# A transformer block on one Trainium2 core: the list schedule behind the attention starts 2.1 slots later, and its rule and table of numbers change

## The chip, the cores and the metric

The kernel runs on one core of a Trainium2 chip. The core has five engines with instruction queues of their own: TensorE (PE) for matmuls, VectorE (DVE), ScalarE (ACT), GpSimd (POOL) and SyncE (SP), which here does nothing but issue transfers (DMA). Each engine works through its queue in the order in which the program was written down, and waits at an instruction until what it needs is there. So the order of instructions on each engine is fixed before the kernel runs, and the order is what this change alters.

The metric is the device time of one execution in microseconds (us); lower is better. Three executions of the kernel before took 988.43, 991.43 and 991.93 us, median 991.43.

## The reference

The input x has 2048 rows of 512 numbers. What is computed, with 32 heads of 16 and a window of 256:

```python
mod = (_silu(c) @ w_mod).reshape(c.shape[0], 6, 1, -1)
sa, ca, ga, sb, cb, gb = (mod[:, 0], ..., mod[:, 5])
h = _layernorm(x) * (1 + ca) + sa
q, k, v = ...  # h @ wqkv, split into 32 heads of 16
scores = jnp.einsum("bhqd,bhkd->bhqk", q, k) * (Dh ** -0.5)
mask = (idx[:, None] - idx[None, :] >= 0) & (idx[:, None] - idx[None, :] < W)
p = _softmax(jnp.where(mask, scores, -1e9))
x = x + ga * (einsum("bhqk,bhkd->bhqd", p, v) @ wo)
h = _layernorm(x) * (1 + cb) + sb
x = x + gb * ((_silu(h @ w1) * (h @ w3)) @ w2)      # w1, w3: 512 x 1792, w2: 1792 x 512
```

All of it is float32. The kernel splits an operand into a high and a low part, and a product of two such operands is three matmuls.

## The kernel before, in words

**Attention.** 32 units of work, four heads and one block of 512 query rows each. Unit u is spread over stages: `unit_a` multiplies the normalised rows by the weights of queries and keys (L433), mixes high and low parts on GpSimd (L451) and writes the result through SyncE into a ring of rows laid out for the scores (`ring<-qk`, L456, six transfers of 128 KB). `unit_b` makes a first set of scores (`mx<-ring`, L486), finds each row's maximum on VectorE (L493 to L502), turns it (L508) and puts it into the ring (`ring<-mT`, L517). `unit_c` makes the scores again with the maximum subtracted (L736, L739), applies exponential and mask (L744 to L785), multiplies by the values (L712) and stores the output (`o_dr<-os`, L804). The stages of neighbouring units overlap; a unit takes eight slots of the plan, and a hand-written table gives each step's place in slots. The last unit is number 31; its six row transfers stand at slots 231.45 to 231.79.

**Behind the attention**, for four blocks of 512 rows: `o_sums` loads softmax sums (L1051), takes reciprocals (L1055) and writes them (L1056). `o_part` loads an output tile (L1075) and the spread reciprocals (L1070), multiplies (L1087) and splits into high and low (L1079, L1082). `o_proj` multiplies by the output weights (L1099) and `add_stats` adds x and gathers statistics (L968 to L976). `load_x1` fetches x (L1036), `load_wo` the output weights (L1030). Then the second layer norm (`ln_rstd` L987 to L993, `ln2` L1219 with turns on TensorE L1233).

**Feed-forward.** Two halves of the rows, seven steps each. A step has 14 up products (`ffn`, L1361, six matmuls each; fourteen since the 2 x 2 x 2 block products are done by seven), elementwise work on ACT, VectorE and GpSimd (L1384 to L1413), and 8 down products (L1454). The step's weights are loaded by `load_w` (L1157) and `load_w2` (L1200) and split (ACT L952, GpSimd L953). Each down step overwrites the one down-weight buffer, so the next load of it starts after the last down product of the step before. `half_rows` (L1294, L1302) and `late_job` (L862, L1173, L1187) prepare work for later steps on the side.

**What sets the order.** All steps of the attention with a place below `TS`, in slots, are issued in the order of the places. The others, `fixed`, enter the list scheduler `Sched` at a time `us(t)`; the work behind the attention enters it as operations with an engine, a cost, dependencies and a priority (`key`) that comes from the table `K`. `Sched.deal` takes, at each step, for the engine that is free first, the ready operation of the lowest key. Of `fixed` the row transfers are `urgent`: a transfer `o` that would run when an urgent one is due is put off. `CAPS` limits how many result banks turns (`tp`), up (`up`) and down products (`dn`) may hold at a time. Three things in `K` choose the engine of an instruction (`be`, `by`) and a count per block (`n`); all else are keys and shifts of keys in us, such as `fl`, the distance between steps of the feed-forward, and `w0`, the key of the first weights' load.

```python
    last = [o for o in ops if o[0] >= TS]
    fixed = [(us(t), fn, *KINDS[kind]) for t, _, fn, kind in last]
    urgent = [us(t) for t, _, _, kind in last if kind in ("rows", "qk_rows")]
```

Of the kernel before, what the change touches and what calls it, by code (L numbers as in the profile page):

```python
# [36 lines left out]
         o=(9.93, 10.63), job=(-0.855, 2.493, 10.058))  # L37
# [26 lines left out]
HOP = {"PE": 0.42, "ACT": 0.2, "DVE": 0.15, "POOL": 0.1, "SP": 0.0, "NIL": 0.0}  # L64
SWITCH = 0.2
STRETCH = 3.413
CAPS = dict(tp=1, up=5, dn=5)


def act(n):  # L70
# [39 lines left out]
class Sched:  # L110
# [36 lines left out]
    def deal(self):  # L147
# [4 lines left out]
        mode, wire, lanes, clock = 0, 0.0, [0.0] * 8, Clock()  # L152
        banks, fixed = list(self.banks), list(self.fixed)
        held = dict.fromkeys(CAPS, 0)
        given = dict.fromkeys(CAPS, 0)
        order, self.dealt = [], []
# [8 lines left out]
        while left:  # L165
            best = None
            for e, lst in ready.items():
                t, pick = free[e], None
                for key, seq, o in lst:
                    s = o.est  # L170
                    new = [b for b in o.bank if b.i is None]
                    if new:
                        use = new[0].use
                        if held[use] >= CAPS[use] or (use in INORDER and new[0].n != given[use]):
                            continue
                        at = min(banks)
                        if at == INF:
                            continue
                        s = max(s, at)
                    if o.kb:  # L180

                        b = max(s, t)
                        end = max(wire, b + 1.5) + o.kb / RATE + o.more - QUIET
                        s = max([s] + [u + 0.01 for u in self.urgent if b <= u < end])
                    if s <= t:
                        pick = (t, o)
                        break
                    if pick is None or s < pick[0]:
                        pick = (s, o)
                if pick and (best is None or pick[0] < best[0]):  # L190
                    best = pick
            if fixed and (best is None or fixed[0][0] <= best[0]):

                t, e = max(free[fixed[0][2]], fixed[0][0]), fixed[0][2]
# [7 lines left out]
            elif fixed and (best is None or fixed[0][0] <= best[0]):  # L202
                t, fn, e, occ = fixed.pop(0)
# [5 lines left out]
            s, o = best  # L209
# [11 lines left out]
            if o.kb:  # L221
                s = max(s, lanes.pop(0))
                wire = max(wire, s + 1.5) + o.kb / RATE + o.more
# [29 lines left out]
INF = float("inf")  # L253
RATE = 320.0

QUIET = 1.5
KEY = 1.715
TS = 229.9


def us(t):

    return KEY * (min(t, TW[0]) - TS + TW[2] * max(0.0, min(t, TW[1]) - TW[0]) + TW[3] * max(0.0, t - TW[1]))


TW = (231.0, 241.0, 0.8, 0.65)

KINDS = dict(product=("PE", 0.235), mix=("POOL", 1.25), qk_rows=("SP", 1.2), out=("ACT", 0.5), job=("POOL", 2.0),
             job_dma=("SP", 0.5), scores=("PE", 0.2), top=("DVE", 0.5), parts=("DVE", 0.4), turn=("PE", 0.11), cut=("ACT", 0.16),
# [6 lines left out]

BY = ((("POOL", "POOL"),) * 3 + (("DVE", "DVE"),), (("POOL", "POOL"),) * 3 + (("DVE", "DVE"),),
      (("POOL", "DVE"),) * 3 + (("DVE", "DVE"),), (("POOL", "POOL"),) * 4)
K = dict(be=(('DVE', 'DVE'), ('DVE', 'POOL'), ('DVE', 'POOL'), ('POOL', 'POOL'), ('POOL', 'DVE'),
         ('POOL', 'DVE'), ('DVE', 'DVE')), hr=0.109, de=7.098, wo=-0.159, x1=5.764, xb=-29.382,  # L280
         xl=0.241, os=-0.129, ol=(-15.316, -4.484, -6.572, 4.956), pl=(3.999, 1.87, -4.828,
         102.62), pe=(0.982, -5.962, 56.258, 232.622), o=(1.381, 8.497, 20.124, -0.531), n=(1, 1,
         2, 1), w0=62.113, l2=0.424, f=1.543, fl=40.897, by=((('POOL', 'POOL'), ('DVE', 'DVE'),
         ('DVE', 'POOL'), ('DVE', 'DVE')), (('DVE', 'DVE'), ('DVE', 'POOL'), ('DVE', 'DVE'),
         ('DVE', 'POOL')), (('POOL', 'POOL'), ('POOL', 'DVE'), ('DVE', 'POOL'), ('POOL', 'DVE')),
         (('POOL', 'DVE'), ('DVE', 'POOL'), ('DVE', 'POOL'), ('DVE', 'POOL'))), w=0.559, dn=1.412,
         ds=0.003, l3=-0.027)
@with_exitstack
def block_kernel(ctx: ExitStack, tc: tile.TileContext, x, wqk, wv, wo, w13, w2, c, wmod, out):
    nc = tc.nc  # L290
# [1299 lines left out]
```

## Time and profile before

| | |
|---|---|
| executions | 988.43, 991.43, 991.93 us; median 991.43 |
| profiled execution | 987.77 us, its span 986.0 us |
| TensorE busy | 944.6 us (96%) |
| VectorE, ScalarE, GpSimd busy | 717.9, 554.2, 609.8 us |
| transferred | 141.64 MB, 144 GB/s on the mean |
| granted TensorE clock | 0.990 on the mean |

In rows of the profile, the first number is the start in us from the span's start, the second the busy time of the row, then engine, line, operation, and `out<-in` by the program's names; xN says that N instructions are joined. What stands in square brackets is idle time of the engine just before, and what ended it. SPq is SyncE's queue issuing a transfer; its time is that of issuing, not of the transfer. PEld is the loading of weights into TensorE. The rows of stretches give for each engine the busy time in the stretch, then the granted clock, the share of the DMA engines that was busy, and GB/s. Rows of waits give the total, the count and the longest, in us.

### The profile page before, as it was taken

The numbers are of one execution on the slowest core, as the hardware profiler recorded it, in microseconds if no ns is written. First come the engines' busy times: TensorE is split into PE (matmuls) and PEld (weight loads), VectorE is DVE, ScalarE is ACT, GpSimd is POOL, SyncE is SP. The second block draws the span as 40 slices with busy tenths as digits, with TensorE's granted clock in tenths as the row PEclk, the third lists the DMA queues.
The fourth block names the chain that finished last, engine by engine and source line by source line (L and its number), as shares of the span: only waits on it lengthen the run. The fifth ranks groups of instructions, "written<-read, shape, count | busy, mean of one in ns | idle before, by whom it ended". The sixth has DMA issues, their size and how long they took to land.

```text
span 986.0 us, 17173 instructions
## 1 busy us (share of the span) xinstructions
PE 944.6 (96%) x5316; PEld 717.4 (73%) x5316; DVE 717.9 (73%) x1999; ACT 554.2 (56%) x1252; POOL 609.8 (62%) x775
## 2 busy tenths in 40 slices
PE   5999999999999999997888999999999999999998
PEld 2578777777777776764566778878888888888886
DVE  7775889899989999996467676755568655555455
ACT  3433887787878787874577864333445344433330
POOL 7441787787868686864476588897737555443420
PEclk9999999999999999997999999999999999999999
DMA  8621354444544444435891558765336423312102
GB/s 280 189 87 34 125 187 142 142 141 142 177 150 148 145 150 143 142 131 152 218 268 68 175 169 285 235 206 192 121 96 208 147 73 96 96 59 81 38 22 85
DMA packets 80671, 141.64 MB, mean 144 GB/s; under 512 B 9538, under 2 KB 22338, under 8 KB 80580
## 3 DMA queue, kind: packets, MB, share of 16 engines
q1 hardware_dynamic: 79860, 139.50, 43.8%
q10 hardware_dynamic: 720, 1.05, 0.3%
q8 instruction: 42, 0.69, 0.3%
q14 instruction: 49, 0.40, 0.1%
HBM read 85.72 MB, written 34.61 MB: 122 GB/s over the span
## 4 chain that ended last, share of the span: by engine, by line
PE 74%; POOL 8%; DVE 7%; DMA 6%; issue 2%; ACT 2%; SPq 1%; POOLq 0%; DVEq 0%; ACTq 0%
PE mx L1361 11%; PE st L1361 11%; PE mx L486 8%; PE pj L433 7%; PE st L736 7%; PE st L1454 6%; PE po L712 6%; PE mx L1454 6%; PE pj L1361 4%; PE st L650 3%; PE pj L1454 2%; POOL w L953 2%; POOL pt L764 2%; POOL qk L451 1%; DMA ring<-qk 1%
## 5 line engine op out<-in xcount | busy, mean ns | idle before, releaser
L493 DVE CUSTOM_DVE_ANT_0 junk<-mx,mskq 128x384 bf16<-128x384 f32 (+2 forms) x512 | 256.5, 527 | 35.4 <-PE mx L486 34.1
L953 POOL TENSOR_TENSOR w<-w,w 128x512 fp32r<-128x512 f32 (+2 forms) x56 | 107.7, 1936 | 124.4 <-ACT w L952 93.4
L486 PE MATMUL mx<-ring 96*128 96x384 f32 (+2 forms) x512 | 155.9, 342 | 9.9 <-DMA ring<-qk 6.9
L736 PE MATMUL st<-ring 100*128 100x384 f32 (+2 forms) x512 | 156.3, 346 | 2.8 <-ACT pt L748 1.4
L764 POOL TENSOR_SCALAR_AFFINE_SELECT pt<-pt 128x256 f32<-128x256 f32 x268 | 108.6, 408 | 73.4 <-ACT pt L757 63.1
L433 PE MATMUL pj<-hT,wq 128*128 128x512 f32 x384 | 136.3, 405 | 1.5 <-DVE hT L350 1.2
L486 PEld LDWEIGHTS mx<-ring 96*128 96x128 f32 x512 | 94.1, 190 | 43.5 <-DVE mt L493 25.0
L757 ACT ACTIVATE pt<-st 128x256 f32<-128x256 f32 x268 | 96.1, 386 | 41.9 <-DVE st L754 34.4
L736 PEld LDWEIGHTS st<-ring 100*128 100x128 f32 x512 | 95.8, 190 | 24.8 <-issue 8.0
L712 PE MATMUL po<-pt,vS 128*17 128x384 f32 (+2 forms) x1408 | 96.6, 391 | 1.4 <-POOL pt L764 0.9
L451 POOL TENSOR_TENSOR qk<-qkr,qk 128x512 fp32r<-128x512 f32 x64 | 82.7, 1292 | 15.9 <-ACT qkr L439 15.6
L754 DVE COPY_PREDICATED st<-later,st 128x128 f32<-128x128 uint8 x268 | 72.1, 291 | 10.2 <-PE st L736 6.3
L433 PEld LDWEIGHTS pj<-hT,wq 128*128 128x128 f32 x384 | 71.7, 190 | 8.7 <-DVE hT L350 1.5
L1432 ACT ACTIVATE wq<-g 128x512 fp32r<-128x512 f32 x28 | 17.7, 633 | 91.0 <-PE st L1454 31.6
L712 PEld LDWEIGHTS po<-pt,vS 128*17 128x17 f32 x1408 | 33.2, 97 | 47.2 <-issue 21.3
L1392 DVE TENSOR_TENSOR t<-mx,t 128x512 f32<-128x512 f32 x50 | 34.4, 688 | 45.4 <-PE mx L1361 31.0
L1361 PE MATMUL st<-b,w 128*128 128x512 f32 x258 | 64.6, 392 | 0.8 <-DVE b L1258 0.4
L1361 PE MATMUL mx<-b,w 128*128 128x512 f32 x252 | 62.7, 394 | 1.1 <-ACT mx L976 1.1
L748 ACT ACTIVATE pt<-st 128x384 f32<-128x384 f32 (+2 forms) x128 | 52.7, 434 | 17.5 <-DVE st L744 13.9
L1392 DVE TENSOR_TENSOR t<-st,t 128x512 f32<-128x512 f32 x47 | 32.3, 687 | 41.5 <-PE st L1361 23.8
L781 POOL TENSOR_SCALAR_AFFINE_SELECT sm<-sm 128x256 f32<-128x256 f32 x109 | 41.9, 407 | 28.1 <-ACT sm L771 24.1
L1361 PEld LDWEIGHTS st<-b,w 128*128 128x128 f32 x258 | 48.1, 188 | 11.9 <-DVE b L1258 0.8
(265 smaller groups left out, 2088.8 us busy)
## 6 DMA issues: line engine op xcount, KB each, us to landing
ring<-qk SPq DMA_DIRECT2D x192, 128.0 KB
o_dr<-os SPq DMA_DIRECT2D x32, 256.0 KB
w<-wsum SPq DMA_DIRECT2D x14, 512.0 KB
w<-w2g SPq DMA_DIRECT2D x14, 512.0 KB
jb<-in_w SPq DMA_DIRECT2D x24, 256.0 KB
wraw<-in_w SPq DMA_DIRECT2D x7, 768.0 KB
w<-wraw SPq DMA_DIRECT2D x14, 384.0 KB
vS<-in_wmod SPq DMA_DIRECT2D x20, 256.0 KB
```

What stands on the lines that cost most here:

```text
L433: nc.tensor.matmul(v["ps"], WQ[g][w][:, n // 3], hTp(i, n // 3, b * BT, BT), start=(n == 0), stop=(n == 3 * KC - 1))
L451: nc.gpsimd.tensor_tensor(out=v[n], in0=v["raw"], in1=v[1].bitcast(F32), op=ALU.subtract)
L486: nc.tensor.matmul(v[i][:, :n], queries(NS, a, gq, 1), keys(NS, hh, a, k0, gq + 1 - k0), start=True, stop=True)
L493: nc.vector.tensor_tensor_reduce(out=junk[:, :n], in0=v[i][:, :n], in1=mskq[:, 3 * P - n:], scale=1.0, scalar=-3e38, op0=ALU.add, op1=ALU. ...
L712: nc.tensor.matmul(po[32 * i:32 * i + DH + 1, qb * P:(qb + nq) * P], vS[:, kb, 4 * g + i], pts[i // 2][:, i % 2, c0:c0 + nq], start=first, ...
L736: nc.tensor.matmul(ps[:, :nq], keys(NM, hh, a, kb, 1), queries(NM, a, kb, nq), start=True, stop=not plus)
L754: nc.vector.copy_predicated(ps[:, 0], later, ps[:, 2])
L757: nc.scalar.activation(held[u, j, a][:, hh, :2], v[j, a, hh][:, :2], AF.Exp, scale=SCALE)
L764: nc.gpsimd.affine_select(out=pt[:, :, 2 * m], in_=pt[:, :, 0], **w)
L953: sch.op(eng, lambda: on_eng(eng).tensor_tensor(out=lo(), in0=src(), in1=hi().bitcast(F32), op=ALU.subtract), 0.06 + 0.0024 * n if eng == ...
L1361: nc.tensor.matmul(ps(bk), WT[s, n][w][:, col], BB[t, k][r], start=start and c == 0, stop=stop and c == 5, skip_group_check=True)
L1454: nc.tensor.matmul(ps(bk), tiles[hk + (h,)][:, i * P:(i + 1) * P], w2_of(last, y, f), start=(m == 0), stop=(m == 5))
```

## The change

The diff:

```diff
-CAPS = dict(tp=1, up=5, dn=5)
+CAPS = dict(tp=4, up=3, dn=5)
...
                         b = max(s, t)
-                        end = max(wire, b + 1.5) + o.kb / RATE + o.more - QUIET
+                        end = max(wire, b + 1.5) + o.kb / RATE + o.more
                         s = max([s] + [u + 0.01 for u in self.urgent if b <= u < end])
...
-QUIET = 1.5
-KEY = 1.715
-TS = 229.9
+
+TS = 232.0
+TW = (241.0, 1.42, 1.2)
 
 
 def us(t):
-
-    return KEY * (min(t, TW[0]) - TS + TW[2] * max(0.0, min(t, TW[1]) - TW[0]) + TW[3] * max(0.0, t - TW[1]))
-
-
-TW = (231.0, 241.0, 0.8, 0.65)
+    return TW[1] * (min(t, TW[0]) - TS) + TW[2] * max(0.0, t - TW[0])
...
-K = dict(be=(('DVE', 'DVE'), ('DVE', 'POOL'), ('DVE', 'POOL'), ('POOL', 'POOL'), ('POOL', 'DVE'),
...
+K = dict(be=(('POOL', 'POOL'), ('POOL', 'POOL'), ('DVE', 'DVE'), ('POOL', 'DVE'), ('POOL', 'DVE'),
...
```

With `TS` at 232.0 the six row transfers of the last unit are issued before the list schedule begins; before, they were among its urgent transfers. `QUIET` shortened by 1.5 us the time in which a transfer counts as overlapping an urgent one; it is gone. `us` turns slots into us for the plan alone, with other numbers. The whole table `K` is replaced. The set of operations stays the same; six of them move from VectorE to GpSimd. Lines behind 264 have numbers lower by two in the changed kernel.

Up to the first product of the output projection, TensorE's queue is the same in both. Three places differ as follows.

First SyncE's queue round the rows of the last unit, before and then after. `x1a<-in_x` are loads of x, `wqr<-o_dr` loads of softmax sums, `wo<-wog` the output weights, `r_dr<-wqr` writes of reciprocals, `ring<-qk` the rows.

```order
239 L1036 DMA x1a<-in_x 128x512 x2
240 L1051 DMA wqr<-o_dr_75 96x1x128
241 L1051 DMA wqr<-o_dr_76 96x1x128
242 L1051 DMA wqr<-o_dr_77 96x1x128
243 L1036 DMA x1a<-in_x 128x512 x2
244 L1030 DMA wo_7577<-wog 128x512 x4
245 L1056 DMA r_dr_79<-wqr 96x128
246 L456 DMA ring<-qk_7534 16x4x512 x2
247 L456 DMA ring<-qk_7504 16x4x512 x2
248 L456 DMA ring<-qk_7542 16x4x512 x2
```

```order
239 L1034 DMA x1a<-in_x 128x512 x3
240 L454 DMA ring<-qk_7534 16x4x512 x2
241 L454 DMA ring<-qk_7504 16x4x512 x2
242 L454 DMA ring<-qk_7542 16x4x512 x2
243 L1034 DMA x1a<-in_x 128x512
244 L1054 DMA r_dr_79<-wqr 96x128
245 L1028 DMA wo_7626<-wog 128x512 x4
246 L1049 DMA wqr<-o_dr_75 96x1x128
247 L515 DMA ring<-mT 4x4x128 x2
248 L802 DMA o_dr_74<-os 128x512
```

Before, the rows follow four loads of x, three of sums, four of weights and a write; now they follow three loads of x, and the rest comes behind them.

Second SyncE's queue at the store of the last unit's block: `w<-wraw` and `w<-wsum` are the first weights of the feed-forward, `mT<-o_dr` is the last block's load of sums, `qk<-r_dr`, `wq<-r_dr` and `wq<-o_dr` are loads of `o_part`.

```order
286 L804 DMA o_dr_77<-os 128x512
287 L1070 DMA qk_8181<-r_dr_82 128x1x512
288 L1157 DMA w_8218<-wraw 128x2x384
289 L1157 DMA w_8218<-wsum 128x2x512
290 L1070 DMA wq_8237<-r_dr_81 128x1x512
291 L1157 DMA w_8220<-wraw 128x2x384
292 L1051 DMA mT<-o_dr_77 32x1x128
293 L1075 DMA wq_8253<-o_dr_76 128x1x512
294 L1157 DMA w_8220<-wsum 128x2x512
295 L1200 DMA w_8222<-w2g 128x1024
```

```order
289 L802 DMA o_dr_77<-os 128x512
290 L1155 DMA w_8218<-wraw 128x2x384
291 L1155 DMA w_8218<-wsum 128x2x512
292 L1155 DMA w_8220<-wraw 128x2x384
293 L1155 DMA w_8220<-wsum 128x2x512
294 L1049 DMA mT<-o_dr_77 32x1x128
295 L1198 DMA w_8222<-w2g 128x1024
```

The load of sums stood behind three loads of weights and stands behind four now; the loads of `o_part` between them come later.

Third TensorE's queue in an early step of the feed-forward, where down products (`w_8221`) and up products (`b_...`) meet.

```order
2121 L1454 MATMUL mx<-w_8221,qkr 128x512
2122 L1454 MATMUL mx<-w_8222,qkr 128x512
2123 L1454 MATMUL mx<-w_8221,qk_9216 128x512
2124 L1454 MATMUL mx<-w_8221,qk_9154 128x512
2125 L1454 MATMUL mx<-w_8222,qk_9154 128x512
2126 L1454 MATMUL mx<-w_8221,qk_9161 128x512
2127 L1361 MATMUL mx<-b_8213,w_8219 128x512
2128 L1361 MATMUL mx<-b_8213,w_8220 128x512
2129 L1361 MATMUL mx<-b_8214,w_8219 128x512
2130 L1361 MATMUL mx<-b_8215,w_8219 128x512
2131 L1361 MATMUL mx<-b_8215,w_8220 128x512
2132 L1361 MATMUL mx<-b_8216,w_8219 128x512
```

```order
2115 L1359 MATMUL mx<-b_8189,wo_8674 128x512
2116 L1359 MATMUL mx<-b_8189,wo_8675 128x512
2117 L1359 MATMUL mx<-b_8190,wo_8674 128x512
2118 L1359 MATMUL mx<-b_8191,wo_8674 128x512
2119 L1359 MATMUL mx<-b_8191,wo_8675 128x512
2120 L1359 MATMUL mx<-b_8192,wo_8674 128x512
2121 L1452 MATMUL pj<-w_8221,qkr 128x512
2122 L1452 MATMUL pj<-w_8222,qkr 128x512
2123 L1452 MATMUL pj<-w_8221,qk_9241 128x512
2124 L1452 MATMUL pj<-w_8221,qk_9239 128x512
2125 L1452 MATMUL pj<-w_8222,qk_9239 128x512
2126 L1452 MATMUL pj<-w_8221,qk_9253 128x512
```

Before, the eighth of eight down products in a row (six matmuls each) is followed by fourteen up products. Now four downs run in a row, then four in turn with up products of the next step, and ten up products follow those.

More of the change, by code (lines that the diff above doesn't have):

```diff
@@ L278 @@
       (("POOL", "DVE"),) * 3 + (("DVE", "DVE"),), (("POOL", "POOL"),) * 4)
-K = dict(be=(('DVE', 'DVE'), ('DVE', 'POOL'), ('DVE', 'POOL'), ('POOL', 'POOL'), ('POOL', 'DVE'),
[L280 to L287, printed above, removed]
+K = dict(be=(('POOL', 'POOL'), ('POOL', 'POOL'), ('DVE', 'DVE'), ('POOL', 'DVE'), ('POOL', 'DVE'),
+         ('DVE', 'POOL'), ('POOL', 'DVE')), hr=-1.052, de=-0.252, wo=-0.137, x1=18.277,
+         xb=-21.268, xl=-0.271, os=-0.144, ol=(-3.949, -1.752, -81.893, -20.883), pl=(11.002,
+         -5.243, -8.426, 246.381), pe=(4.316, -7.47, 16.772, 58.525), o=(0.368, 12.612, 16.311,
+         -4.213), n=(1, 2, 2, 1), w0=11.454, l2=-3.717, f=10.245, fl=5.014, by=((('DVE', 'POOL'),
+         ('POOL', 'DVE'), ('DVE', 'POOL'), ('DVE', 'POOL')), (('DVE', 'POOL'), ('POOL', 'DVE'),
+         ('DVE', 'POOL'), ('POOL', 'POOL')), (('POOL', 'DVE'), ('POOL', 'POOL'), ('POOL', 'DVE'),
+         ('POOL', 'DVE')), (('POOL', 'POOL'), ('DVE', 'DVE'), ('DVE', 'POOL'), ('DVE', 'POOL'))),
+         w=0.381, dn=1.96, ds=0.065, l3=0.578)
 @with_exitstack
```

## The prediction

> **What bounds the kernel now.** I read the views in this order: busy time by engine, waits of TensorE, stretches of 5 us round the longest wait, then the rows of each engine inside it. The first view gives the engine that a gain must reach, the second the place where that engine stands still for a reason that this change touches.
>
> ```profile
> PE 944.6 (96%) x5316; PEld 717.4 (73%) x5316; DVE 717.9 (73%) x1999; ACT 554.2 (56%) x1252; POOL 609.8 (62%) x775
> ...
> PE mx L486 <- DMA ring<-qk: 6.9, 3, 5.9
> PE mx L1233 <- ACT wqr L1219: 2.0, 1, 2.0
> ...
> 425.00:605.00 180.00, 160.11 (x855) 117.27 (x848) 124.05 (x275) 114.81 (x235) 110.35 (x113) 0.95 0.60 182
> ...
> 585.00:980.00 395.00, 394.38 (x1708) 319.76 (x1708) 237.83 (x323) 150.70 (x237) 221.93 (x167) 1.00 0.39 130
> ```
>
> TensorE is busy for 944.6 of 986.0 us, so 41.4 us is all that an order alone can win back by filling gaps. From 585 to 980 (the feed-forward part) it misses 0.6 of 395 us: nothing is to be won there, only lost. From 425 to 605, the passage from attention to feed-forward, it misses 19.9 us, and there the list schedule works. The largest wait in it is 5.9 us for `ring<-qk`, the rows of the last unit. The chain that ended last runs through the same place:
>
> ```profile
> 442.63 6.27 DMA wo<-wog
> 448.97 0.55 SPq L456
> ...
> 449.89 2.57 DMA ring<-qk
> ...
> 452.81 0.66 PE mx L486
> ```
>
> The chain passes through a load of the output weights before it reaches the rows: the queue was full of other things. SyncE's rows say of what, first for the unit before, then for the last one:
>
> ```profile
> 426.89 3.89 SPq L456 DMA_DIRECT2D ring<-qk  x6
> ...
> 436.73 1.80 SPq L1036 DMA_DIRECT2D x1a<-in_x  x2
> ...
> 441.11 1.00 SPq L1036 DMA_DIRECT2D x1a<-in_x  x2
> 442.15 1.85 SPq L1030 DMA_DIRECT2D wo<-wog  x4
> ...
> 444.57 5.86 SPq L456 DMA_DIRECT2D ring<-qk  x6
> ...
> 439.90 1.28 POOL L451 TENSOR_TENSOR qk<-qkr,qk 128x512 fp32r<-128x512 f32 x1
> ...
> ring<-qk SPq DMA_DIRECT2D x12, 128.0 KB
> x1a<-in_x SPq DMA_DIRECT2D x4, 256.0 KB
> wo<-wog SPq DMA_DIRECT2D x4, 256.0 KB
> ```
>
> The last rows' data were ready when the second mix on GpSimd ended, 439.90 + 1.28 = 441.2, yet SyncE began to issue them at 444.57 and finished at 450.43. Ahead of them stand four loads of x and four of the output weights, 8 x 256 KB = 2.0 MB.
>
> What it does to TensorE is in its own rows and in the stretches:
>
> ```profile
> 446.25 0.69 PE L736 MATMUL st<-ring 100*128 100x384 f32 x1
> 452.81 0.66 PE L486 MATMUL mx<-ring 96*128 96x384 f32 x1 [5.87 <-DMA ring<-qk]
> 453.26 0.52 PE L736 MATMUL st<-ring 100*128 100x384 f32 x1
> ...
> 459.37 0.34 PE L736 MATMUL st<-ring 100*128 100x384 f32 x1
> ...
> 445.00:450.00 5.00, 1.94 (x20) 0.76 (x9) 1.55 (x7) 1.40 (x3) 0.00 (x0) 0.78 0.81 258
> 450.00:455.00 5.00, 2.19 (x8) 2.05 (x9) 1.24 (x5) 0.65 (x3) 0.05 (x1) 0.57 0.27 82
> 455.00:460.00 5.00, 5.00 (x39) 3.64 (x38) 2.92 (x11) 3.59 (x9) 4.02 (x6) 0.75 0.16 58
> ...
> 485.00:490.00 5.00, 4.80 (x42) 3.23 (x41) 2.80 (x5) 2.15 (x8) 2.60 (x3) 1.00 1.07 279
> ...
> 505.00:510.00 5.00, 3.65 (x17) 2.68 (x15) 4.27 (x13) 3.48 (x7) 4.89 (x4) 1.00 1.04 302
> 510.00:515.00 5.00, 3.38 (x9) 2.32 (x10) 2.17 (x1) 5.00 (x10) 3.75 (x3) 0.71 0.57 174
> ```
>
> All engines stand idle with TensorE: from 450 to 455 VectorE works 1.24 us of 5, GpSimd 0.05. Nothing else advances in the stall, so its length is on the path. And the matmul of L736 lasts 0.52 us after it and 0.34 us again from 459.37: the granted clock is down to 0.57 and 0.75 in these stretches.
>
> **The change part by part.** The sum is made against the profiled execution, 987.77 us (986.0 span and 1.8 round it). The median of the runs is 991.43 (988.43 to 991.93), 3.7 above; I carry the difference over to that median. About 0.5%, 5 us, is what a measurement of this kernel can tell from no change.
>
> *Rows first.* The order shows 0.75 MB (three loads of x) instead of 2.0 MB ahead of the rows; the fourth load of x, four loads of weights and three small loads now stand behind them. I estimate when the rows land: issue ends about 1.2 us after the mix, at 442.4; by the chain a last piece lands (0.55 + 0.37 + 2.57 =) 3.5 us after its issue begins, so near 445.5. TensorE runs out of other work at 446.25 + 0.69 = 446.94. So the rows come 1.4 us early and the whole wait of 5.87 us goes. From below: if 1.75 MB (0.75 of x, 0.25 of a store, 0.75 of rows) must all move at the 258 GB/s of 445 to 450, beginning only when the mix ends, the last lands near 448.2; a wait of 1.2 us stays and 4.6 are won. Taken: -5.9, since the loads of x are issued from 436.73, before the mix ends; ends -4.6 and -5.9.
>
> *The clock.* Between 452.81 and 459.37 TensorE worked at about half its clock for 6.6 us; without the wait before it the same work takes half of that, 3.3 us. In 455 to 460 TensorE is busy 5.00 of 5.00 and no other engine over 4.02, so it set the pace there. Ends 0 (if VectorE, which runs nearly full in the unit's normal pace, takes over at once) and -3.3. Taken: -3.3.
> [...]
>
> *The moved loads.* 1.25 MB now go behind the rows, at 258 GB/s some 5 us of transfer, in the stretch where DMA was at 0.27 and 0.16 of its capacity. Those two stretches are the cover, and it holds: the loads of weights are first used by the splits of GpSimd, and only the output projection, after 480, needs them. If the cover is gone they delay the loads that follow, by up to 5 us; that is a rival below. Cost taken: 0.
>
> *The last block's sums.* The layer norm behind the attention waits for a small load of the last block's sums; its issue now stands behind one more load of 512 KB (four instead of three):
>
> ```profile
> w<-wsum SPq DMA_DIRECT2D x14, 512.0 KB
> ...
> 497.11 0.69 SPq L1051 DMA_DIRECT2D mT<-o_dr  x1
> ...
> 504.38 0.94 DVE L1055 RECIPROCAL mT<-mT 32x128 f32<-32x128 f32 x1 [2.67 <-DMA mT<-o_dr]
> ```
>
> VectorE waited 2.67 us for that load, and TensorE then 2.0 us for the normalised rows. 512 KB at 302 GB/s take 1.7 us. Ends 0 (the extra load shared the wires before as well, it was issued right behind) and +1.7. Taken: +1.6.
>
> *The other moves between attention and feed-forward.* Output groups of the projection go from six to four inside the attention, transposes come four in a row, six instructions move from VectorE to GpSimd. From 505 to 515 TensorE misses 10 - 3.65 - 3.38 = 3.0 us in this work. At best all of it goes, -3; at worst it doubles, +3. GpSimd, at 4.89 of 5 there, gets work and VectorE loses it, so I take +1.
>
> *The feed-forward's order.* Down products move behind all up products of their step, and then run four in a row and four in turn with the next step's ups. Same instructions on a TensorE that is full in both: 0, hidden as long as the split weights come in time. Here is that cover, for the tightest step I found and for a late one:
>
> ```profile
> 631.16 0.32 SPq L1200 DMA_DIRECT2D w<-w2g  x1
> 642.42 2.54 POOL L953 TENSOR_TENSOR w<-w,w 128x512 fp32r<-128x512 f32 x2
> 650.74 1.56 PE L1454 MATMUL pj<-w,wq 128*128 128x512 f32 x6
> ...
> 692.24 1.10 PE L1454 MATMUL st<-w,qk 128*128 128x512 f32 x4
> 693.13 0.32 SPq L1200 DMA_DIRECT2D w<-w2g  x1
> 698.13 5.33 POOL L953 TENSOR_TENSOR w<-w,w 128x512 fp32r<-128x512 f32 x3 [3.14 <-ACT w L952]
> 712.71 1.56 PE L1454 MATMUL st<-w,wq 128*128 128x512 f32 x6
> ```
>
> Fourteen groups of ups lie between two sets of downs, 712.71 - 693.3 = 19.4 us, 1.39 each; the change leaves ten, 13.9 us. The down weights need from issue to the end of the split 644.96 - 631.16 = 13.8 us at worst. It just fits.
>
> Sum: -5.9 - 3.3 + 0 + 1.6 + 1 + 0 = -6.6, thus 981.2 for an execution like the profiled one and 991.4 - 6.6 = 984.8, said as 985.0, for the median.
>
> **The rivals.**
> 1. *The gain is given back on the wires.* DMA is at 1.07 and 1.04 of its capacity from 485 on. If the attention ends 9 us sooner and the loads behind it do not, TensorE waits for them, at the same moment as before. For it: the loads for output and feed-forward follow in one queue. Against it: from 445 to 460 the wires have room (0.81, 0.27, 0.16). At worst it takes the 1.25 MB's 5 us, leaving -1.6: 989.8; with half of it 987.3. [...]
> 2. *The feed-forward starves.* The window of 13.9 us against the need of 13.8: if the split comes late by d in each of 12 steps, TensorE loses 12 d. With d = 1 us the 6.6 are lost and 5.4 more, 996.8; the point from which this decides against the change is d = 0.55. For it: GpSimd's fillings between two splits, which are ordered anew. Against it: the late step needs 698.13 + 5.33 - 693.13 = 10.3 us at most, and 13.9 remain. So 990 to 1000, and 997 as its time.
> 3. *The rows are still late.* A store and three loads of x stand ahead, and the rows' pieces are issued one by one. If the wait shrinks only to 3 us, the clock falls still and its term goes: -2.9 + 0 + 1.6 + 1 = -0.3, 991.
> 4. *Everything goes well.* The sums aren't later, and the transfers in the middle shrink: -9.2 - 3, 979.
>
> **How the numbers follow.** The forecast's own course 0.36, the good case 0.14, given back 0.20, rows late 0.10, starved 0.20. From the forecast's course and the good case nearly all is faster by over 0.5%; a little of the former (0.05) falls within, and of the given back a part (0.05) counts as faster. Faster: 0.36 + 0.14 - 0.05 + 0.05 = 0.50. Slower: of the starved 0.17, and 0.03 of the late rows, where the wait moves but does not shrink: 0.20. The same: 0.05 + 0.15 + 0.07 + 0.03 = 0.30. The forecast's own range is -9.2 to -3.3, 982 to 988. The whole range goes from 978, the good case with a little to spare, to 997, the starved one; beyond lie at most 2 in 10.
>
> **What would show each step.** Rows: in SyncE's view the six pieces end before 443, and the wait of L486 on `ring<-qk` is under 1.5 us; wrong if it is over 3. Clock: no stretch between 445 and 460 under 0.9. Sums: the reciprocal of L1055 comes some 6 to 8 us before 504.38. Wires: rival 1 if the stretches over 1.0 begin as before while TensorE waits more for `o` or `wq`. Feed-forward: from 585 on TensorE misses under 1 us; rival 2 if waits on GpSimd's splits appear at L1454, with a sum over 5 us. The prediction as a whole is wrong if the wait goes and the total does not follow.

## The result, and the profile after

The changed kernel takes 990.78 us (median of 20 runs, 988.31 to 993.83), the kernel before 990.09 (20 runs, 987.99 to 993.08, the three of the prediction among them): ratio 1.0009, 95% interval 0.9998 to 1.0020. So it is nothing that can be told from no change, where 985.0 (978 to 997) had been forecast with a gain of 6.6 us. The time lies in the range, but the gain isn't there.

The profiled execution after has a span of 990.0 us, 4.0 longer than the one before. First TensorE's wait for the rows from the view of waits over the whole span (us in total, times, longest), then two stretches (length, busy time of TensorE, its weight loads, VectorE, ScalarE and GpSimd, granted clock, share of the DMA engines, GB/s).

```profile
PE mx L484 <- DMA ring<-qk: 2.3, 2, 1.7
```

```profile
425.00:605.00 180.00, 162.90 (x879) 120.64 (x879) 120.21 (x280) 118.52 (x244) 120.41 (x122) 0.96 0.59 187
585.00:980.00 395.00, 391.39 (x1682) 315.62 (x1681) 237.79 (x317) 149.36 (x234) 218.49 (x165) 1.00 0.38 127
```

The longest wait for the rows fell from 5.9 to 1.7 us. From 425 to 605 TensorE misses 17.1 us instead of 19.9, and its mean clock there is 0.96 instead of 0.95. From 585 to 980 it misses 3.6 us, where it missed 0.6.

SyncE's queue round the rows, after:

```profile
439.39 2.25 SPq L1034 DMA_DIRECT2D x1a<-in_x  x3
441.73 3.83 SPq L454 DMA_DIRECT2D ring<-qk  x6
445.61 0.58 SPq L1034 DMA_DIRECT2D x1a<-in_x  x1
...
447.22 1.85 SPq L1028 DMA_DIRECT2D wo<-wog  x4
```

The rows now stand ahead of five loads of 256 KB, and are issued in 3.83 us instead of 5.86.

To see where the gain goes, I take a mark ahead of the change: the store of the attention that comes just before those rows. Up to it TensorE does the same matmuls in the same order in both; the store is at 436.20 before and at 438.85 after, so 2.65 us of the 4.0 are scatter between two executions. Times below are counted from the mark. First the mark and the four last stores of the attention, before and then after, then the first down product of the feed-forward and TensorE's last row in each.

```profile
436.20 0.43 SPq L804 DMA_DIRECT2D o_dr<-os  x1
...
456.14 0.43 SPq L804 DMA_DIRECT2D o_dr<-os  x1
...
470.58 0.58 SPq L804 DMA_DIRECT2D o_dr<-os  x1
...
480.23 0.38 SPq L804 DMA_DIRECT2D o_dr<-os  x1
...
491.38 0.37 SPq L804 DMA_DIRECT2D o_dr<-os  x1
...
589.58 1.64 PE L1454 MATMUL st<-w,wq 128*128 128x512 f32 x6
...
981.94 0.39 PE L1454 MATMUL st<-w,wqr 128*128 128x512 f32 x1
```

```profile
438.85 0.43 SPq L802 DMA_DIRECT2D o_dr<-os  x1
...
452.27 0.44 SPq L802 DMA_DIRECT2D o_dr<-os  x1
...
468.20 0.42 SPq L802 DMA_DIRECT2D o_dr<-os  x1
...
478.48 0.34 SPq L802 DMA_DIRECT2D o_dr<-os  x1
...
491.91 0.33 SPq L802 DMA_DIRECT2D o_dr<-os  x1
...
590.25 3.04 PE L1452 MATMUL mx<-w,wq 128*128 128x512 f32 x12
...
985.86 0.39 PE L1452 MATMUL st<-w,wqr 128*128 128x512 f32 x1
```

| counted from the mark | before | after | shift |
|---|---|---|---|
| first store | 19.94 | 13.42 | -6.5 |
| second | 34.38 | 29.35 | -5.0 |
| third | 44.03 | 39.63 | -4.4 |
| fourth, the end of the attention | 55.18 | 53.06 | -2.1 |
| first down product | 153.38 | 151.40, less 2.74 for two more groups of ups ahead of it | -4.7 |
| last matmul | 545.74 | 547.01 | +1.3 |

So 6.5 us are won at the first store, 4.4 of them are lost again by the end of the attention, the projection and layer norm give some back, 4.7 stand at the door of the feed-forward, and that loses 6.0. In the sets of down products the same count jumps at three places only: +3.3 at the fourth set, +1.3 at the fifth, +1.1 at the seventh; from the eighth set on there is nothing. The first two of them lie in the stretch in which weights for later steps are prepared on the side; the last of these writes is issued at 723.7.

**Inside the attention** late masks on VectorE start the loss, and the clock makes most of it. VectorE's rows and TensorE's:

```profile
473.20 0.94 DVE L1053 RECIPROCAL mT<-mT 32x128 f32<-32x128 f32 x1 [0.77 <-DMA mT<-o_dr]
474.07 1.50 DVE L1080 TENSOR_TENSOR o<-qk,o 128x512 fp32r<-128x512 f32 x1
475.50 0.47 DVE L752 COPY_PREDICATED st<-later,st 128x128 f32<-128x128 uint8 x2
...
477.37 0.41 PE L710 MATMUL po<-pt,vS 128*17 128x128 f32 x8 [1.75 <-POOL pt L762]
```

A mask of the attention (L752) stands behind a reciprocal that waits for a load, and behind work of the output projection; the mask feeds ScalarE, GpSimd and then TensorE, which stands for 1.75 us. At 457.36 the same stands in VectorE's queue, a reciprocal of 0.94 us ahead of a mask, and TensorE waits 1.03 us for what follows it. Round each of these two waits the granted clock falls to half, from 458.67 to 465.50 and from 479.15 to 482.56 (rows under the clock, below). That is 10.2 us at half clock between the first and the fourth store, where the kernel before has 1.3 us, up to 457.48. The difference is worth (10.2 - 1.3) / 2 = 4.5 us at the most, an estimate as large as the whole loss of 4.4. Of the 6.5 us at the first store up to 3 are of the same kind, since the kernel before works at half clock ahead of it (443.82 to 447.23, and 452.81 to 456.14). No run moves VectorE's work alone, so this cause is read from the rows and not tested.

**In the feed-forward** ScalarE is late. SyncE, ScalarE and TensorE at the fourth set:

```profile
670.95 2.81 SPq L1185 DMA_DIRECT2D wsum<-e  x2
673.86 0.39 SPq L1155 DMA_DIRECT2D o<-wsum  x1
...
677.79 1.06 ACT L950 ACTIVATE o<-o 128x1024 fp32r<-128x1024 f32 x1 [2.47 <-DMA o<-wsum]
678.76 1.13 ACT L1382 ACTIVATE g<-t 128x512 f32<-128x512 f32 x2
679.79 0.58 ACT L1393 ACTIVATE t<-pj 128x512 f32<-128x512 f32 x1
...
680.42 2.85 PE L1359 MATMUL pj<-b,w 128*128 128x512 f32 x6 [2.29 <-ACT t L1393]
...
680.54:683.95 3.41, 3.41 (x9) 2.67 (x10) 1.88 (x3) 1.36 (x3) 3.41 (x4) 0.50 0.33 123
```

A load of weights for a later step follows the write of sums that GpSimd finished late; the cast of that load stands at the head of ScalarE's queue, and the copy that frees a result bank of TensorE (L1393) stands behind it. TensorE waits 2.29 us and does its next six matmuls in 2.85 us instead of 1.56 (at 650.32), for the granted clock is at half from 680.54 to 683.95 (last row). Nothing there waits for the down weights. The two smaller jumps come with waits of 0.58 us for a copy on ScalarE (L1397, at 715.40) and of 0.59 us for an addition on VectorE (L1390, at 769.11); these free result banks too.

### The profile page after: what moved, and what is told of

It is laid out like the page before. It is cut to its first block, busy times and chain, and to the rows that moved or that the text cites. A ratio compares the mean times of both kernels' runs of the same rounds, so it can differ in the third digit from the quotient of the medians.

```text
span 990.0 us, 17171 instructions
## 1 busy us (share of the span) xinstructions
PE 947.3 (96%) x5316; PEld 719.0 (73%) x5316; DVE 712.8 (72%) x1993; ACT 555.0 (56%) x1252; POOL 615.7 (62%) x781
## 4 chain that ended last, share of the span: by engine, by line
PE 74%; DVE 8%; POOL 6%; DMA 4%; ACT 4%; issue 3%; SPq 0%; POOLq 0%; DVEq 0%; ACTq 0%
PE st L1359 10%; PE mx L1359 9%; PE mx L484 8%; PE pj L431 7%; PE st L734 7%; PE po L710 7%; PE mx L1452 6%; PE st L1452 6%; PE st L648 4%; PE pj L1359 3%; PE pj L1452 2%; POOL pt L762 2%; POOL qk L449 1%; DMA ring<-qk 1%; DVE junk L491 1%
## 5 line engine op out<-in xcount | busy, mean ns | idle before, releaser
L951 POOL TENSOR_TENSOR w<-w,w 128x512 fp32r<-128x512 f32 (+2 forms) x56 | 99.4, 1791 | 52.4 <-ACT w L950 43.6
L1402 POOL TENSOR_TENSOR t<-t,t 128x512 f32<-128x512 f32 x28 | 37.2, 1329 | 76.8 <-DVE t L1390 76.8
L752 DVE COPY_PREDICATED st<-later,st 128x128 f32<-128x128 uint8 x268 | 72.2, 291 | 15.4 <-PE st L734 10.2
L950 ACT ACTIVATE w<-w 128x512 fp32r<-128x512 f32 (+2 forms) x56 | 43.5, 786 | 45.4 <-DMA w<-wraw 27.4
L1359 PE MATMUL st<-b,w 128*128 128x512 f32 x252 | 63.1, 392 | 1.2 <-ACT st L974 0.8
L1390 DVE TENSOR_TENSOR t<-st,t 128x512 f32<-128x512 f32 x47 | 32.3, 688 | 40.6 <-PE st L1359 22.8
L1359 PE MATMUL mx<-b,w 128*128 128x512 f32 x246 | 61.3, 393 | 0.0
L1390 DVE TENSOR_TENSOR t<-mx,t 128x512 f32<-128x512 f32 x46 | 31.6, 688 | 39.1 <-PE mx L1359 19.3
```

The source lines that it names most:

```text
L752: nc.vector.copy_predicated(ps[:, 0], later, ps[:, 2])
L951: sch.op(eng, lambda: on_eng(eng).tensor_tensor(out=lo(), in0=src(), in1=hi().bitcast(F32), op=ALU.subtract), 0.06 + 0.0024 * n if eng == ...
L1359: nc.tensor.matmul(ps(bk), WT[s, n][w][:, col], BB[t, k][r], start=start and c == 0, stop=stop and c == 5, skip_group_check=True)
```

## The experiments

All times are medians of five rounds, beside runs of the kernel before on the same chip (988.7 to 990.0 us in each). Ratios are to those runs.

The question was where a gain that the waits show has gone. Theory A: the feed-forward in its new order loses what the passage before it gains. Its rival: the passage itself gives the gain back, so that the order of the feed-forward doesn't matter.

**The two halves exchanged.** Keys of the feed-forward and CAPS from one kernel, the rest from the other.

```diff
 # after_ffn_of_before, from the changed kernel
-CAPS = dict(tp=4, up=3, dn=5)
+CAPS = dict(tp=1, up=5, dn=5)
-K: be=..., hr=-1.052, de=-0.252, f=10.245, fl=5.014, w=0.381, dn=1.96, ds=0.065, l3=0.578
+K: be=..., hr=0.109, de=7.098, f=1.543, fl=40.897, w=0.559, dn=1.412, ds=0.003, l3=-0.027
```

> The changed kernel with the feed-forward's keys (fl, f, dn, ds, w, de, l3, hr, be) and the limits of banks of the kernel before; the passage behind the attention keeps the changed keys. Theory A, the change is two parts that cancel, some 5 us won up to the 28th group of the feed-forward and some 6 us lost behind it: this gives about 985 us, ratio 0.995, and TensorE misses under 1 us from 600 to 980. Theory B, the loss in the feed-forward comes from the passage (transfers and splits that start at another time), whatever the feed-forward's own order: about 990 us, ratio 1.000, with waits of L1359 on ScalarE between 640 and 780.

984.22 us, ratio 0.9947 (0.9929 to 0.9965): 0.5% faster than the kernel before and 0.62% or 6.1 us than the changed one (1.0009). From 585 to 980 TensorE misses 0.8 us. Theory A holds, though the passage isn't quite the same: from 425 to 605 TensorE is busy for 164.71 us, and for 162.90 in the changed kernel.

```profile
425.00:605.00 180.00, 164.71 (x880) 120.28 (x879) 124.40 (x281) 118.67 (x246) 122.36 (x125) 0.96 0.62 189
585.00:980.00 395.00, 394.16 (x1703) 318.90 (x1701) 230.26 (x323) 148.16 (x234) 216.94 (x159) 1.00 0.38 127
```

The reverse, the same lines put into the kernel before:

> The other half: the kernel before with the changed keys of the feed-forward and the changed limits of banks. Theory A: about 996 us, ratio 1.006, with TensorE waiting 3 to 6 us for ScalarE between 600 and 800 and the 5.9 us for the rows unchanged. Theory B: about 990 us, ratio 1.000, no such waits.

1002.29 us, ratio 1.0132 (1.0110 to 1.0154), twice what theory A gave. The wait for the rows is 7.6 us there instead of 5.9, and the waits of L1361 between 425 and 600 show more of the rest: the keys also order the feed-forward's first steps, among the projection.

```profile
PE st L1361 <- ACT b L1256: 2.8, 1, 2.8
PE st L1361 <- DVE t L1392: 2.6, 1, 2.6
```

So the halves don't add up as numbers, but their signs stand.

**The later start alone**, with the old table: once with everything of the change but K and CAPS, once with TS alone.

```diff
 # before_ts_only
-TS = 229.9
+TS = 232.0
```

> The kernel before, table and limits unchanged, with the later start of the list schedule, the changed us() and without QUIET: only the rows come first, and what the plan makes of that. If the prediction's first two terms carry through to the end: the wait for the rows under 2 us and -9 us, about 981, ratio 0.991. If the gain is worn away behind the rows, in the last unit, by VectorE's work for the output projection: the wait goes, but -5 to -2 us, about 985 to 988. If the rows' wait costs nothing: 990.

> The kernel before with TS = 232.0 and nothing else changed (QUIET, us() and the table as before). The rows are issued ahead of the list; the rest of the plan is dealt anew. Theory C: the wait for the rows goes, the end stays within 4 us of before, 986 to 994, and where the gain goes is in the passage. The first two terms carried through: 981.

990.76 us, ratio 1.0018 (1.0002 to 1.0033), and 991.57, ratio 1.0019 (1.0003 to 1.0035). In neither do the waits of TensorE from 425 to 600 name the rows (`ring<-qk`) any more; in both the largest wait from 500 to 600 is for ScalarE, first in the one, then in the other:

```profile
PE mx L1359 <- ACT t L1393: 5.7, 1, 5.7
...
PE mx L1361 <- ACT t L1395: 4.7, 1, 4.7
```

A wait of 5.9 us went and one of about 5 us came, 90 us later, in the feed-forward's first steps.

**The rows alone, in the old order.** The order dealt for the kernel before is kept on every engine, and only transfers are moved behind the rows.

```diff
 # before_rows_swap, ahead of the issue of the dealt order
+    late_ = [o.fn for o in sch.dealt if o.kb and o.tag in ("wo", "x1")
+             and order.index(o.fn) < at_row]
+    order = rest_[:cut_] + late_ + rest_[cut_:]     # cut_: behind the last row
```

> The kernel before, in which only SyncE's queue differs: the four loads of x and the four of output weights stand behind the last unit's rows instead of ahead of them; all other engines keep their order. The wait for the rows should fall from 5.9 to under 1 us and the next store of the attention come 6 to 7 us sooner. Theory C, the gain is worn away behind, since the queues were ordered for a late attention: at the end -4 to 0 us, 985 to 989. The prediction's first two terms carried through: -9 us, 980. Theory D, the loads that now come behind the rows take it all back or more: 989 or above.

991.73 us, ratio 1.0020 (1.0007 to 1.0033). But something else had moved: three small loads of sums, which had stood behind the loads of x, went up in SyncE's queue ahead of four stores of the attention. Their issue alone takes 2.5 us there (3.34 - 0.87), and the next store is as much late, in this kernel first, then in the kernel before:

```profile
398.97 3.34 SPq L1051 DMA_DIRECT2D wqr<-o_dr  x4
...
403.91 0.44 SPq L804 DMA_DIRECT2D o_dr<-os  x1
```

```profile
398.99 0.87 SPq L1051 DMA_DIRECT2D wqr<-o_dr  x1
401.44 0.43 SPq L804 DMA_DIRECT2D o_dr<-os  x1
```

At the store just ahead of the rows the delay is 3.4 us (439.61 against 436.20). That run thus doesn't tell what it was meant to. It did show ScalarE waiting 3.5 us for the output weights; moving their casts was tried on it:

> before_rows_swap (992), in which ScalarE's casts of the output weights and GpSimd's splits of them stand behind eight more operations of ScalarE; nothing else changes place. In before_rows_swap ScalarE waited 3.5 us for the load of these weights and TensorE 3.7 us for the exponential behind the cast. Theory F, the in-order ScalarE turned the late load into a stall of the attention: the wait of L736 on L748 falls under 1 us and the time to 985 to 988. If what wears the gain lies elsewhere (VectorE, the last block's sums, transfers): 990 to 992.

991.98 us, ratio 1.0017 (1.0002 to 1.0032), with the same late store in it: nothing to be told. With the first two loads of x left ahead of the rows the small loads stay where they were, and the two runs were made again.

```diff
 # before_rows_swap2
-             and order.index(o.fn) < at_row]
+             and order.index(o.fn) < at_row][2:]
```

> The kernel before, in which on SyncE alone two loads of x and the four of output weights stand behind the last unit's rows; nothing else moves (in before_rows_swap three loads of sums had moved too, ahead of an earlier unit's rows, and cost 2.5 us there). Theory F: the wait for the rows falls under 3 us, a wait of some 3 us for ScalarE takes its place (exponential behind the cast of the output weights), and the time is 986 to 990. The prediction's first two terms carried through: 981.

988.71 us, ratio 0.9991 (0.9977 to 1.0006). The wait for the rows fell to 2.6 us, and a new one came, as theory F had it:

```profile
454.86 1.29 ACT L952 ACTIVATE wo<-wo 128x512 fp32r<-128x512 f32 x2 [2.79 <-DMA wo<-wog]
...
456.58 0.44 PE L736 MATMUL st<-ring 100*128 100x384 f32 x1 [2.77 <-ACT pt L748]
```

The output weights, now behind the rows, land after ScalarE has come to their cast; the exponential behind it waits, and TensorE with it. Then the casts, with the splits behind them, eight operations later:

> before_rows_swap2 with ScalarE's casts and GpSimd's splits of the output weights behind eight more operations of ScalarE. Theory F: the wait for ScalarE falls under 1.5 us, and the time by some 2 us against before_rows_swap2, to 984 to 988. If the casts don't matter: as before_rows_swap2.

986.68 us, ratio 0.9970 (0.9956 to 0.9984), and the wait of L736 on L748 is 0.9 us at most. Theory F holds: with the order of ScalarE unchanged the row's gain is eaten by a cast, and 0.21% (0.9991 - 0.9970) or 2 us come back when that is moved (the two intervals overlap by 0.0007, so this size is rough). With that 3.0 us (0.0030 x 990) of the 9.2 forecast for the rows and the clock come out. In the profiled execution the clock falls even so, though over its 12 runs the mean granted clock is 0.991, and 0.990 in the runs of the kernel before beside them:

```profile
448.90 0.66 PE L486 MATMUL mx<-ring 96*128 96x384 f32 x1 [2.35 <-DMA ring<-qk]
...
450.00:455.00 5.00, 5.00 (x33) 4.06 (x35) 3.14 (x14) 2.28 (x6) 1.63 (x4) 0.50 0.84 254
```

**The rows late again, in the best order.** All loads of x and the output weights ahead of the rows in after_ffn_of_before; the other engines keep their order.

```diff
 # best_rows_late: the three fns of rows are held back from the hand order
+    order = first_ + held_ + [fn for fn in order if fn not in first_]   # first_: 4 loads of x, 4 of wo
```

> The reverse on the kernel after_ffn_of_before (984): only SyncE's queue differs, all four loads of x and the four of output weights stand ahead of the rows again. If the rows' place is what the gain of that kernel is made of: wait of L484 on the rows back to 4 to 7 us, and 989 to 993. If its gain comes from the rest of the table (projection, layer norm, engines): 984 to 986 although the wait is back.

994.27 us, ratio 1.0040 (1.0026 to 1.0053), against 0.9947 for its parent: 0.9% or 9 us for the place of the rows. The wait is back:

```profile
PE mx L484 <- DMA ring<-qk: 5.7, 1, 5.7
```

```profile
425.00:605.00 180.00, 159.19 (x836) 114.27 (x836) 114.99 (x266) 113.45 (x234) 113.66 (x116) 0.92 0.58 178
```

From 425 to 605 TensorE is busy 5.5 us less than in the parent (164.71 - 159.19), and the mean clock is 0.92 instead of 0.96. Over the runs of the two the mean granted clock is 0.982 (8) and 0.989 (6), so up to 0.007 x 990 = 7 of the 9 us are half clock. The prediction's price of the rows, 9.2 us, is thus about right in an order that was made for early rows, and about 1 us in one that was made for late ones.

**The feed-forward.** First the limit of banks, up=5 in the changed kernel.

> The changed kernel with up=5 instead of up=3, nothing else. If the loss in the feed-forward comes from the three banks (TensorE has no free bank as soon as ScalarE is late with a copy): about 985 us, ratio 0.995, no waits of L1359 on L1393 or L1397 over 1 us. If it comes from the order of casts and copies on ScalarE, which up=5 leaves: 989 to 991 us, ratio 1.000.

989.90 us, ratio 1.0011 (0.9999 to 1.0023). The waits of 600 to 800 fell to 1.0 us, but the passage got new ones, the largest of them 2.6 us for VectorE, since the limit is also one of the deal's rules: a loss moved, none removed.

Then the keys of the down products alone, put into the changed kernel, and the reverse.

```diff
 # after_dn
-K: dn=1.96, ds=0.065
+K: dn=1.412, ds=0.003
```

> The changed kernel with the two keys of the down products of the kernel before (dn, ds): eight downs in a row and fourteen ups in a row again, steps still 5 us of key apart, banks 4, 3, 5. If the alternation of ups and downs makes the loss: 984 to 986. Under theory G it matters only as far as it moves casts and loads: 987 to 991, with waits on ScalarE left.

985.84 us, ratio 0.9955 (0.9940 to 0.9970). TensorE's longest wait from 600 to 800 is now:

```profile
PE mx L1359 <- ACT t L1397: 0.4, 1, 0.4
```

> The kernel before with the changed keys of the down products alone (dn, ds): downs and ups in turn, steps 41 us of key apart as before. If the alternation of downs and ups alone costs: 993 to 996. If it costs only with the late work put last by the changed keys: 988 to 991.

993.92 us, ratio 1.0046 (1.0028 to 1.0064). So these two keys, which put four of the eight downs in turn with ups, cost about 5 us with either table (0.54% or 5.3 us, and 0.46% or 4.6 us). In this kernel the wait from 600 to 800 is another, for an addition on VectorE, which frees a result bank:

```profile
PE mx L1361 <- DVE x1a L1459: 2.8, 1, 2.8
```

The six matmuls behind it take 2.49 us, where six of them take 1.56 at 767.68, and the granted clock is 0.98 on the mean from 700 to 800, so that wait and clock together make an estimated 2.8 + 0.02 x 100 = 4.8 us, about as much as the run shows.

Why the keys cost was asked in three ways. The preparation of late weights first in the plan:

```diff
 # after_jobs_first, in late_job
-               sch.op("POOL", ..., 0.37, key + 0.3 * i, ...)
+               sch.op("POOL", ..., 0.37, key + 0.3 * i - 900.0, ...)
-        dma(..., key + 2, [name], [dk], 256)
+        dma(..., key - 898.0, [name], [dk], 256)
```

> The changed kernel, in which only the plan's priority of the late weights' preparation (late_job: sums on GpSimd and the write) is put first; the changed keys, with steps 5 us apart, had put it behind all else. Theory E, the feed-forward's waits come from late sums, late loads, and casts on ScalarE that stand and wait for them ahead of the copies that free TensorE's banks: the waits of L1359 on ScalarE between 640 and 780 go, 985 to 986, ratio 0.996. If the order of down and up products or the banks make them: 989 to 991.

989.38 us, ratio 0.9997 (0.9982 to 1.0011). The waits from 600 to 800 fell to 1.2 us, but the deal of the first steps changed as well and has a new wait of 2.8 us for ScalarE: not decided by the time.

The casts of weights four operations later on ScalarE, with nothing else moved but their splits:

> The changed kernel, in which ScalarE's casts of the feed-forward's up weights, and GpSimd's splits of them, stand behind four more of the feed-forward's operations of ScalarE (never behind TensorE's first use); TensorE, VectorE and SyncE keep their order. Theory G, the feed-forward's loss comes from casts that wait for their load at the head of ScalarE's queue: TensorE's waits between 640 and 780 under 1 us in all and 985 to 987. If it comes from the order of up and down products on TensorE: they stay, 989 to 992.

996.09 us, ratio 1.0069 (1.0046 to 1.0092): a miss. The waits on ScalarE in 600 to 800 grew to 5.4 us in four, the longest of them

```profile
PE mx L1359 <- ACT t L1393: 2.4, 1, 2.4
```

A blind shift moves casts ahead of other copies, which is the likely reason but isn't shown; theory G in that form, that standing later is enough, falls. Last, the 64 late sums on GpSimd left out (the late steps then multiply by other numbers):

> The changed kernel without the sums on GpSimd in the late preparation of weights (64 small operations left out; the copies to and from memory stay, so the late steps multiply by other numbers). If the late sums on GpSimd make the feed-forward's loss: TensorE's waits between 640 and 780 under 1 us, 985 to 987. If the alternation of ups and downs makes it by itself: 989 to 991.

986.61 us, ratio 0.9973 (0.9961 to 0.9985), 0.36% or 3.6 us below the changed kernel. The longest wait from 600 to 800 is 0.6 us, for VectorE (L1390).

So 3.6 of the 6 us need the late sums on GpSimd. The jam in the changed kernel is the two together: the order of downs and ups, and sums that come late in it. The last of the 16 writes behind the sums (`wsum<-e`) is issued at 704.1 in the changed kernel, at 681.0 in after_dn and at 681.4 in the kernel before. In what way the order makes the sums late (the deal of GpSimd, SyncE and ScalarE differs as a whole between after and after_dn) stays open. In before_dn_of_after the last write is issued at 681.3, so the price there isn't one of late sums; why the addition on VectorE is late there stays open too.

## Why the prediction was wrong, point by point

- *Rows first*, -5.9: the mechanism was right, and the size a little outside its ends of -4.6 and -5.9: the wait went from 5.87 to 1.71 us, which is -4.2. The rows were issued by 445.56, 442.9 when the 2.65 us of scatter are taken off; 442.4 had been estimated. The first matmul on them came at 449.62, 447.0 without the scatter, where 445.5 had been estimated for their landing, and TensorE had run out of work 1.7 us sooner. In an order made for it the place of the rows is worth 9 us (best_rows_late), as much as the sum of the first two terms.
- *The clock*, -3.3: failed. The sentence "without the wait before it the same work takes half of that" took for granted that without this wait no fall is left. TensorE's two waits after the change, and the stretches round them:

```profile
449.62 0.41 PE L484 MATMUL mx<-ring 96*128 96x384 f32 x1 [1.71 <-DMA ring<-qk]
...
458.95 0.69 PE L734 MATMUL st<-ring 100*128 100x384 f32 x1 [1.03 <-ACT pt L755]
```

```profile
448.43:451.84 3.41, 2.23 (x13) 1.97 (x14) 1.72 (x7) 1.54 (x5) 0.45 (x2) 1.00 0.88 273
455.26:458.67 3.41, 2.28 (x9) 1.27 (x8) 3.36 (x10) 0.98 (x4) 2.10 (x4) 1.00 0.21 50
458.67:465.50 6.83, 6.55 (x35) 3.97 (x36) 4.16 (x18) 3.84 (x10) 4.54 (x5) 0.50 0.58 160
...
479.15:482.56 3.41, 3.41 (x20) 2.64 (x24) 1.45 (x3) 2.24 (x6) 2.39 (x3) 0.50 1.01 307
```

  The longer wait left the clock at 1.00; round the shorter one it falls to half for 6.8 us, and behind the wait of 1.75 us at 477.37 for 3.4 us more. The kernel before has the same two lengths:

```profile
443.82:447.23 3.41, 3.12 (x25) 1.15 (x17) 2.62 (x11) 1.54 (x4) 0.81 (x2) 0.50 0.88 282
...
450.65:457.48 6.83, 4.67 (x15) 4.02 (x15) 2.90 (x11) 2.60 (x8) 2.46 (x4) 0.50 0.19 62
```

  So between these two profiles the clock gives nothing back in the attention. The prediction had also misread its stretches: half clock ended at 457.48, not at 459.37, so that TensorE worked at it for 4.7 us behind the wait and not 6.6, worth 2.3 us and not 3.3; and the 3.4 us ahead of the wait weren't seen as half clock. The runs say the same as the profiles: the mean granted clock is 0.988 in the 20 runs of the changed kernel and 0.990 in the 102 runs of the kernel before beside the experiments, 0.002 x 990 = 2 us at the most, and the other way. In best_rows_late against its parent the clock does fall with the long wait (0.92 against 0.96 from 425 to 605): the term exists, but not every order collects it.
- *The moved loads*, 0: failed as a general statement. "Only the output projection, after 480, needs them" left out that their casts stand in ScalarE's queue between exponentials from 454 on. In the old order this took back 2 us (before_rows_swap2 against rows_swap2_casts); in the changed kernel the casts at 453.30 and 459.17 waited for no load. The cover named was one of the wires; the cost was one of an in-order engine.
- *The last block's sums*, +1.6: didn't come. The reciprocal behind that load came at 501.59 (504.38 before), 5.4 us sooner without the scatter, and waited for no load:

```profile
501.59 0.93 DVE L1053 RECIPROCAL mT<-mT 32x128 f32<-32x128 f32 x1
```

- *Other moves*, +1: mis-sized, and looked for at the wrong place. Between the first store and the end of the attention 4.4 us went, in half clock round waits for VectorE's late masks; the passage after it gave 2.6 back. I had looked at GpSimd's load, not at what stands ahead of the masks.
- *The feed-forward's order*, 0: this is the step that decided. "Same instructions on a TensorE that is full in both: 0, hidden as long as the split weights come in time" failed by 6.0 us between the two traces, and by 6.1 us between the runs of the two orders (1.0009 against 0.9947). The down weights did come in time; the cover that broke was the copies that free the banks, twice on ScalarE and once on VectorE, with half clock behind the longest of the three waits.
- *The rivals.* The first had the right time (989.8) by a mechanism that the runs don't show: with the same transfers behind the rows, after_ffn_of_before keeps its gain. The second named the stage that decided, the feed-forward, but not the wait (L1359 on ScalarE instead of L1454 on splits), and its "point from which this decides", 0.55 us in each of 12 steps, was three jams instead. Of the third the clock came true without its condition: the wait shrank to 1.71 us and not to 3, and the clock fell still. That both could hold at once, the rows' gain and the feed-forward's loss, was in no case: the rivals were taken to exclude one another, and a sum of a true gain and a true loss looks like nothing.

The engineering result is after_ffn_of_before, 984.22 us: the changed start and passage with the old order of the feed-forward.

## What to carry to other kernels

When a stall is taken out of a schedule that was tuned round it, ask of each in-order engine which instruction it reaches next, and what that one waits for: here the gain went to the first cast, mask or copy that was on time only because of the stall (the cast in before_rows_swap2 stood 2.79 us, and TensorE 2.77 us behind it). When one edit changes a table for several stages, price each stage on its own and let the prices add, since a gain in one and a loss in another end as "no change". And an engine that is full in a long stage is no proof that its order is free (TensorE was busy for 394.38 of 395 us, and the new order lost 6.0): what frees its result banks is the cover to be named. The clock's share is better taken from the mean over many runs than from two traces.

## What the runs showed of the hardware that was not expected

TensorE's clock fell to half round waits far shorter than the 5.87 us of the kernel before: round one of 2.35 us in rows_swap2_casts (0.50 from 450 to 455), and round one of 1.03 us in the changed kernel (0.50 from 458.67 to 465.50), where one of 1.71 us nine microseconds earlier had left it at 1.00 (448.43 to 451.84). So in these traces the length of a wait alone doesn't tell whether the clock falls.

In the clock records of the traces of the two kernels the falls and returns lie whole multiples of 3.413 us apart. Behind 400 us, half clock begins in the changed kernel at 458.67, 479.15, 533.76 and 680.54, which is 6, 22 and 65 such steps after the first, and it lasts two steps the first time (TensorE busy for 6.55 of 6.83 us) and one step each time after. In the kernel before it begins at 443.82, 450.65, 512.09 and 549.64, 2, 20 and 31 steps after the first. In each of these two traces all falls and returns (but the end of the trace) lie on one such grid; counted from the start of the span, one trace's grid lies 1.2 us beside the other's.

The wait of 1.71 us lay across an edge of the grid, 448.43, and left TensorE busy for 2.52 and 2.23 us of the two steps. But busy time doesn't sort the steps either: the clock fell behind steps with 2.28 us busy (455.26 to 458.67) and, in the kernel before, with 2.91 (440.41 to 443.82), and didn't behind one with 1.96 (571.31 to 574.72) and, in the kernel before, one with 2.03 (532.57 to 535.98). What in a step decides stays open. In the 20 runs of the changed kernel the mean granted clock goes from 0.983 to 0.993; whether the place of the grid has a part in that wasn't shown.

Where the same instructions are issued in the same order, two profiled executions were 2.65 us apart at the mark: differences of this size between two traces say nothing unless they are counted from a common instruction.
